# A Strassen-Winograd MLP in fp32: product 5 of the first layer halved once more, and its inner weight sums listed in a stream of their own

## The chip, the core and the metric

The kernel runs on one core of a Trainium2 chip. TensorE (PE) multiplies matrices, VectorE (DVE) and GpSimd (POOL) add tensors, ScalarE (ACT) copies and applies functions, SyncE (SP) issues the DMAs that move data between HBM and the core's SBUF. Matmuls write into the banks of PSUM, and DVE and ACT read them from there. The metric is the device time of one execution in microseconds (us); the median of several runs is given, and lower is better.

## What is computed

Performer attention on q, k, v (8 batches, 8 heads, 576 rows of 64), then a Fourier mixing, then a layer norm and an MLP with a hidden width of 2048. All of it is in fp32. Cut to what matters here:

```
x  = attention(q, k, v, omega)              # (8, 576, 512)
u  = x + real(fft(fft(x, axis=1), axis=2))
un = (u - mean(u)) / sqrt(var(u) + 1e-6)
out = u + maximum(un @ w_ch1, 0) @ w_ch2    # 512 -> 2048 -> 512
```

The last line is 4608 rows (tokens) through two matrix products. The change lies in the first of them, `un @ w_ch1`.

## The kernel before, in words

Up to about 421 us the kernel does the attention and the mixing, and the first 512 tokens of the MLP plainly. The other 4096 tokens go through the MLP in eight blocks of 512, j = 0 to 7, from 421 us to the end. Each block has a first layer and a second one.

**Two levels of halving.** A layer's product of two matrices is cut into 2 x 2 halves and done with seven products in place of eight, after Strassen and Winograd: the operands are sums of halves, and the results are added up into the four cells C11, C12, C21, C22 of the result. These are the outer products, numbered 1 to 7. In the first layer they are done in the order `ORDER1 = (1, 6, 5, 2, 7, 3, 4)`, in block 0 in `ORDER0 = (1, 2, 6, 5, 7, 3, 4)`. Each outer product is either

- done "twice" halved: it is itself cut into 2 x 2 halves and done as seven leaves of four matmuls 128 x 128 x 128 (line L1454 in the first layer, L1815 in the second), with inner sums of its weights and of its tokens; or
- done "single": four quarters of four matmuls with 256 columns each (L1586), with no inner sums.

`single(j)` says which. In block 0 all products but the first are single, in blocks 1 to 7 only product 5 is. The second layer is done twice halved throughout.

**What a product of the first layer leaves.** `hid` holds the four cells, each of 2 x 2 tiles of 128 x 512. For a product of leaves, ACT saves partial results (L1479) and copies seeds into banks (L1486), and DVE adds bank and saved part into a cell (L1497, L1401, L1506, L1477). For a single product, ACT copies each quarter's bank into the cell (L1540), and product 5's quarter has one more user: `u4_of`, DVE at L1550, adds bank and C21 into C12, and only then is the bank free. That sum, C12 = C22 + C21, is called u4 here. Product 7's and 3's results are added onto it.

**Sums on SBUF tiles.** All of them are written by a helper, `add`, and have one line, L1419. It lets the planner choose POOL or DVE. Through it go the sums of hidden cells (`hid<-hid`), the sums of hidden tiles for the second layer's leaves (`sums`, three buffers a product, of which the first is used a second time), the outer weight sums `so5`, `so6`, `so3` and the one for product 7, which replaces a part of `w1` in place, and the inner weight sums.

**The inner weight sums.** Each twice halved outer product i of the first layer needs four sums of the quarters of its outer weights: s1, s2, s4, and one that replaces the quarter a21 in place. s1, s2 and s4 are written into a ring of four spare buffers in `rx` and stored to DRAM from there, as `w1l` (L1674, 256 KB each). Every block from 1 on loads them again as `wx` (L1712), in turn with the second layer's leaf weights `wl<-w2l` (L1721), through 12 buffers. The function `w1_sums` lists all of this in one stream: first the outer sums, then for each product in `ORDER0`, as soon as block 0 has done that product's matmuls (a wait for `("first", 0, i)`), its four inner sums. Before block 1's token sums for such products are listed, `token_sums(1)` waits for all the stores.

**What sets the order.** The instructions of each engine are put down in an order that a planner (`Listing.run`) works out ahead of time. It takes steps from several streams (`halves` with the products and their sums, `load_leaves`, `late_norms`, `late_turns`, `w1_sums` ...), each step with an engine, an assumed duration, waits, and a due time made of `due(j, layer, i)` and a `bias`. Of the steps that could begin at about the earliest time it takes the one that is due first. In its model DVE and POOL never add on SBUF operands at the same time. The order thus fixed is run as it stands: each engine does its list in order, and waits on semaphores for what others make. The DMAs named here are all issued from SP's queue, in the order of its list.

In the second layer the outer products go in the order 4, 1, 2, 6, 5, 3, 7. Their results are collected in `part` (L1793 on DVE, L1835 and L1857 on ACT), and added onto the residual `ur` (L1864, POOL or DVE). The tokens of the next block are normed meanwhile (POOL at L1045 to L1047), turned (DVE, L984), stored as `turned` and loaded as `unT` (L1000).

Of the kernel before, what the change touches and what calls it, by code (L numbers as in the profile page):

```python
# [15 lines left out]
ALU = mybir.AluOpType  # L16
# [20 lines left out]
PE, ACT, DVE, POOL, SP, NONE = "pe", "act", "dve", "pool", "sp", "none"  # L37
# [255 lines left out]
def kernel(  # L293
# [10 lines left out]
    nc = tc.nc  # L304
# [880 lines left out]

    def single(j):

        return (5,) if j else ORDER0[1:]

    def twice(j):  # L1190
        return tuple(i for i in ORDER1[1:] if i not in single(j))
# [27 lines left out]
    def token_sums(j):  # L1219
        if j == 1:  # L1220
            yield Step(NONE, after=tuple(("w1l", i, n) for i in twice(1) for n in (5, 6, 3)))
        for i in twice(j):
            for m, op in enumerate(inner_tokens(j, i)):
                yield Step(
                    DVE, 0.28, after=(("tt", j),), makes=("tokens", j, i) if m == 3 else None, port=True,
                    bias=due(j, 0, i) - 5.0,
                )
                op()
# [94 lines left out]
    def sums_left(a11, a12, a21, a22, s1, s2, s4):  # L1323

        return (
            (s1, a21, a22, ALU.add),
            (s2, s1, a11, ALU.subtract),
            (a21, a11, a21, ALU.subtract),
            (s4, a12, s2, ALU.subtract),
        )  # L1330
# [13 lines left out]
    def weights_of(j, i, n):  # L1344
        if i == 1 and n in (5, 6, 3, 7):
            return w1s[:, (5, 6, 3, 7).index(n)]
        if n in (1, 2, 4, 7):
            d, f = {1: (0, 0), 2: (1, 0), 4: (1, 1), 7: (0, 1)}[n]
            return outer_weights(i)[:, d, GW * f : GW * f + GW]
        return wxs[j, i, n]  # L1350
# [54 lines left out]
    def cell_of(c, f, t):  # L1405
        return hid[:, c, f, t]
# [7 lines left out]
    def add(o, l, r, op, engines=(POOL, DVE), **kw):  # L1414
        n = math.prod(o.shape[1:]) / 512
        step = Step({e: {POOL: 1.3, DVE: 0.65}[e] * n + 0.05 for e in engines}, port=True, **kw)
        yield step
        eng = nc.gpsimd if step.eng == POOL else nc.vector
        eng.tensor_tensor(out=o, in0=l, in1=r, op=op)  # L1419
# [5 lines left out]
    def first_of(j, i):  # L1425
# [91 lines left out]
        def last_cell(f, t):  # L1517
            o = cell_of(C22, f, t)
            after = ("h", j, 7, f, t), ("h", j, "u4", f, t)
            yield from add(o, o, cell_of(C21, f, t), ALU.add, after=after, makes=("h", j, "sum", f, t), bias=due(j, 0, 4) - due(j, 0, 5) - 1)  # L1520
            yield Step(ACT, 0.6, 0.1, makes=made(f, t))
            nc.scalar.activation(out=o, in_=o, func=AF.Relu)  # L1522

        if i == 5:
            for f in range(2):
                for t in range(2):
                    yield Fork(last_cell(f, t))
        bank = ("bank",)
        if i in single(j):
            def cells(n, f, c):  # L1530
# [112 lines left out]
    def w1_sums():  # L1643

        a = {n: outer_weights(n) for n in (1, 2, 7, 4)}
        for i in (2, 4):
            for d in range(2):
                for f in range(2):
                    yield Step(NONE, makes=("sum", i, d, f))

        def part(w, d, f):
            return w[:, d, GW * f : GW * f + GW]

        spare = rx[:].rearrange("p i n b q -> p (i n b q)")

        def inner(m, i):
            raw = [weights_of(0, i, n) for n in (1, 2, 7, 4)]
            new = {}
            for k, n in enumerate((5, 6, 3)):
                at = (3 * m + k) % 4 * GW  # L1660
                new[n] = spare[:, at : at + GW]
            ops = sums_left(*raw, *(new[n] for n in (5, 6, 3)))
            for k, (o, l, r, op) in enumerate(ops):
                n = (5, 6, 7, 3)[k]
                turn = 3 * m + (0, 1, 2, 2)[k] - 4
                free = (("stored", turn),) if n != 7 and turn >= 0 else ()
                yield from add(o, l, r, op, (POOL, DVE), after=free, makes=("wx", 0, i, n) if n != 7 else ("so", i, 7), bias=due(1, 0, i) - 40)
            for k, n in enumerate((5, 6, 3)):
                yield Fork(stored(i, 3 * m + k, n, new[n]))

        def stored(i, turn, n, w):
            after = ("wx", 0, i, n), ("wx", 0, i, {5: 6, 6: 3}.get(n, n))
            yield Step(SP, 0.5, 2.5, after=after, kb=256, makes=("stored", turn))
            nc.sync.dma_start(w1l[i][(5, 6, 3).index(n)], w)  # L1674
            yield Step(NONE, makes=("w1l", i, n))

        parts = (0, 1), (0, 0), (1, 0), (1, 1)
        def outer(i, l, r, op, user):
            for d, f in parts:
                yield from add(  # L1680
                    *(part(w, d, f) for w in (outer_weights(i), l, r)), op, (POOL, DVE), makes=("sum", i, d, f),
                    bias=due(0, 0, user) - 6,
                )

        yield Step(NONE, after=(("us", B - 1), "converted"))
        yield from outer(5, a[7], a[4], ALU.add, 6)
        yield from outer(6, so[5], a[1], ALU.subtract, 6)
        yield Step(NONE, after=tuple(("op", n) for n in range(NPLAIN)))
        yield from outer(7, a[1], a[7], ALU.subtract, 7)
        yield from outer(3, a[2], so[6], ALU.subtract, 3)  # L1690
        for m, i in enumerate(i for i in ORDER0 if i in twice(1)):
            yield Step(NONE, after=((("first", 0, i), "leaves"),))
            yield from inner(m, i)
            for n in (1, 2, 4):
                yield Step(NONE, makes=("so", i, n))
# [9 lines left out]
    def load_leaves():  # L1705
        for j in range(NTB):
            for i in twice(j):
                for n in (5, 6, 3):
                    yield Step(SP, 0.45, 2.6, take=("wl",), after=(("w1l", i, n),), kb=165, makes=("wx", j, i, n),
                               bias=due(j, 0, i) - 14)  # L1710
                    wx = late.tile([128, GW], F32, name="wx", tag="wl", bufs=NWL)
                    nc.sync.dma_start(wx[:], w1l[i][(5, 6, 3).index(n)])  # L1712
                    wxs[j, i, n] = wx
            for i in order(j):
                for l in PARTS:
                    yield Step(
                        SP, 0.45, 2.6, take=("wl",), after=(("w2l", i),), kb=165, makes=("wl", j, i, l),
                        bias=due(j, 1, i) - 14,
                    )
                    wl = late.tile([128, 4, 128], F32, name="wl", tag="wl", bufs=NWL)  # L1720
                    nc.sync.dma_start(wl[:].rearrange("p f m -> p (f m)"), w2l[i][STORED.index(l)])  # L1721
                    wls[j, i, l] = wl
# [190 lines left out]
    def due(j, layer, i):  # L1913
        order_ = order(j) if layer else ORDER1 if j else ORDER0
        return LEAF * (98 * j + 49 * layer + 7 * order_.index(i))
# [4 lines left out]
    def wash():  # L1920

        yield Step(POOL, 0.5)
        zero = late.tile([P, DM], BF16, name="junk", tag="junk", bufs=1)
        nc.gpsimd.memset(zero[:], 0.0)
        taken = []
        for i in range(len(CLEAN)):
            yield Step(PE, 0.25, take=("clean",))
            b, ps = got()
            taken.append(b)
            nc.tensor.matmul(ps, lhsT=zero[:, 0:128], rhs=zero[:], start=True, stop=True)  # L1930
        yield Step(NONE, give=tuple(taken), makes="washed")

    def halves():
        yield Step(NONE, after=("washed",))
        for j in range(NTB):
            for i in ORDER1 if j else ORDER0:
                yield Step(NONE, take=("set",))
                yield Fork(first_of(j, i), due(j, 0, i))
            yield Fork(read_up(j))
            yield Fork(left_sums(j), 0.0)  # L1940
            cells = {}
            yield Fork(second_of(j, cells))
            for i in order(j):
                yield Step(NONE, take=("set",))
                yield Fork(product_of(j, i, cells), due(j, 1, i))

    def late_norms():
        for j in range(1, NTB):
            yield from block_norms(j, late)

    def late_turns():
        for j in range(1, NTB):
            yield from normed(j, late)

    listing.run([wash(), late_turns(), late_norms(), halves(), load_leaves(), token_sums(0), w1_sums()])


# [28 lines left out]
```

## Time and profile before

| what | value |
|---|---|
| median of 3 runs | 1149.73 us (1147.95 to 1150.81) |
| profiled execution | 1150.66 us, span 1148.9 us, mean granted clock of PE 0.996 |
| PE busy | 1125.8 us, 98% |
| DVE busy | 875.2 us, 76% |
| ACT busy | 542.7 us, 47% |
| POOL busy | 410.5 us, 36% |
| DMA | 219 GB/s in the mean over the span |

The profile is one execution, taken by the hardware profiler. A row of a timeline or of the chain begins with its start in us from the span's begin and its length; rows of one kind that follow each other are drawn together ("x24" are 24 of them), and what stands in brackets is the idle time before it and what ended that. A fp32 matmul gives two records, so a leaf of four matmuls shows as x8. PE's records are modelled at their ends and overlap by a little, so the pitch from one start to the next is the time of a leaf, not the length of its row. A row of a table by windows gives the window, its length, the busy time and the number of instructions of PE, PE's weight loads, DVE, ACT and POOL, then the granted clock of PE (1.00 is full), the DMA share and GB/s. "Issue" as a releaser means that the profile shows no event that ended the wait. Names of tiles are the program's: `sums` are the second layer's sums, `wl` its weights, `tt` and `unT` tokens of the first layer, `so` and `w` its weights.

### The profile page before, as it was taken

How to read it: one execution, taken by the hardware profiler on the slowest of the kernel's cores; microseconds unless marked ns; L12 is line 12 of the kernel's file. 1: busy time of each engine (PE TensorE's matmuls, PEld its weight loads, DVE VectorE, ACT ScalarE, POOL GpSimd, SP SyncE). 2: the span in 40 equal slices, each digit the busy share in tenths (PEclk: the TensorE clock that was granted, in tenths of full speed). 3: DMA queues.
4: the chain of work that ended last, by engine and by line, in shares of the span. 5: the costliest groups of instructions: out<-in, count | busy, mean ns of one | idle time of the engine just before them, and what ended most of it. 6: DMA issues, size and time to landing. Idle time of an engine off the chain costs nothing.

```text
span 1148.9 us, 33814 instructions
## 1 busy us (share of the span) xinstructions
PE 1125.8 (98%) x13472; PEld 1042.1 (91%) x13472; DVE 875.2 (76%) x1704; ACT 542.7 (47%) x1639; POOL 410.5 (36%) x420
## 2 busy tenths in 40 slices
PE   8999999999999999989999999999999999999998
PEld 7888888879878868989999999999999999999998
DVE  6999899987676645487787777777678688678676
ACT  7998898856444227614424423423423422522311
POOL 2443444455471206720610610520430440340171
PEclk9999999999999999989999999999999999999999
DMA  7866766675663255686796697698598698598476
GB/s 237 233 188 186 212 197 177 194 228 166 204 192 109 86 152 161 202 290 224 230 341 214 197 338 232 184 300 272 170 297 286 178 286 294 181 269 294 146 217 206
DMA packets 184508, 251.97 MB, mean 219 GB/s; under 512 B 52000, under 2 KB 82976, under 8 KB 184352
## 3 DMA queue, kind: packets, MB, share of 16 engines
q1 hardware_dynamic: 183856, 249.56, 70.3%
q8 instruction: 107, 1.75, 0.6%
q14 instruction: 49, 0.40, 0.1%
q10 hardware_dynamic: 496, 0.26, 0.1%
HBM read 206.77 MB, written 47.19 MB: 221 GB/s over the span
## 4 chain that ended last, share of the span: by engine, by line
PE 54%; DMA 3%; issue 1%; DVE 0%; POOL 0%; ACT 0%; SPq 0%; DVEq 0%; POOLq 0%
PE banks L1815 27%; PE banks L1454 23%; PE banks L1586 4%; DMA wl<-w2l 1%; DMA unT<-turned 1%; DVE sums L1419 0%; POOL rstd L1046 0%; ACT u L1049 0%; POOL rstd L1045 0%; DVE part L1793 0%; SPq L1721 0%; SPq L1000 0%; DVE ur L1747 0%; ACT part L1857 0%; ACT banks L1831 0%
## 5 line engine op out<-in xcount | busy, mean ns | idle before, releaser
L1815 PE MATMUL banks<-wl,sums 128*128 128x128 f32 x1792 | 221.6, 277 | 5.2 <-issue 4.8
L1815 PEld LDWEIGHTS banks<-wl,sums 128*128 128x128 f32 x1792 | 211.8, 194 | 5.9 <-issue 5.0
L578 ACT ACTIVATE e<-banks,nmx 128x128 f32<-128x128 f32 x576 | 165.4, 438 | 22.8 <-DVE nmx L561 22.2
L1815 PE MATMUL banks<-wl,hid 128*128 128x128 f32 x1344 | 170.9, 276 | 2.8 <-DMA wl<-w2l 1.4
L1815 PEld LDWEIGHTS banks<-wl,hid 128*128 128x128 f32 x1344 | 160.1, 192 | 4.2 <-ACT s L1788 1.4
L1419 POOL TENSOR_TENSOR hid<-hid 128x512 f32<-128x512 f32 x76 | 100.6, 1335 | 60.3 <-DVE hid L1497 54.9
L561 DVE TENSOR_REDUCE nmx<-banks 128x8 f32<-128x1024 f32 (+1 forms) x96 | 89.3, 951 | 17.2 <-PE banks L618 13.0
L1788 ACT ACTIVATE s<-banks 128x128 f32<-128x128 f32 x112 | 31.1, 277 | 126.0 <-PE banks L1815 109.1
L1864 POOL TENSOR_TENSOR part<-part 128x512 f32<-128x512 f32 x8 | 10.6, 1325 | 223.3 <-ACT part L1857 190.5
L618 PE MATMUL banks<-om,kqT 64*64 64x128 f32 (+1 forms) x2088 | 79.3, 275 | 2.2 <-ACT kv L668 1.5
L1793 DVE TENSOR_TENSOR part<-banks,s 128x128 f32<-128x128 f32 x112 | 32.2, 289 | 58.8 <-PE banks L1815 58.3
L618 PEld LDWEIGHTS banks<-om,kqT 64*64 64x64 f32 (+1 forms) x2088 | 64.7, 138 | 13.5 <-issue 4.1
L1419 DVE TENSOR_TENSOR sums<-hid 128x512 f32<-128x512 f32 x95 | 74.6, 786 | 1.5 <-ACT hid L1522 1.5
L1454 PE MATMUL banks<-rx,wx 128*128 128x128 f32 x560 | 74.0, 275 | 0.0
L1497 DVE TENSOR_TENSOR hid<-banks,s 128x512 f32<-128x512 f32 x58 | 40.1, 691 | 37.1 <-PE banks L1454 36.0
L1454 PEld LDWEIGHTS banks<-rx,wx 128*128 128x128 f32 x560 | 68.2, 192 | 0.0
L1127 PE MATMUL banks<-unT,w 128*128 128x128 f32 x512 | 65.4, 279 | 1.7 <-DVE qeT L538 1.7
L1586 PE MATMUL banks<-tt,so 128*128 128x256 f32 x288 | 66.3, 379 | 0.0
L467 POOL TENSOR_TENSOR w<-w,raw 128x512 f32<-128x512 f32 x28 | 37.5, 1349 | 77.8 <-DVE raw L461 77.8
L1419 DVE TENSOR_TENSOR hid<-hid 128x512 f32<-128x512 f32 x84 | 59.9, 760 | 6.2 <-ACT hid L1540 6.2
L1127 PEld LDWEIGHTS banks<-unT,w 128*128 128x128 f32 x512 | 60.2, 192 | 4.5 <-issue 2.3
L1401 DVE CUSTOM_DVE_ANT_0 hid<-banks,s 128x512 f32<-128x512 f32 x63 | 43.4, 690 | 26.2 <-PE banks L1454 23.2
(194 smaller groups left out, 2398.9 us busy)
## 6 DMA issues: line engine op xcount, KB each, us to landing
wl<-w2l SPq DMA_DIRECT2D x392, 256.0 KB, 5.1
wx<-w1l SPq DMA_DIRECT2D x105, 256.0 KB, 4.1
raw<-in_moe_w_ch_dram SPq DMA_DIRECT2D x32, 512.0 KB, 4.3
kq<-in_k_dram SPq DMA_DIRECT2D x32, 288.0 KB, 4.8
kq<-in_q_dram SPq DMA_DIRECT2D x32, 288.0 KB, 4.6
vd<-in_v_dram SPq DMA_DIRECT2D x32, 288.0 KB, 5.4
u<-us SPq DMA_DIRECT2D x36, 256.0 KB, 2.5
ur<-us SPq DMA_DIRECT2D x36, 256.0 KB, 4.2
```

What stands on the lines that cost most here:

```text
L467: eng.tensor_tensor(out=dst, in0=dst, in1=lof, op=ALU.add)
L561: nc.vector.tensor_reduce(nmx[:, :, 0:num], pps[:, :, 0 : MF * num].rearrange("p b (c m) -> p b c m", m=MF), axis=AX.X, op=ALU.max, negate ...
L578: nc.scalar.activation(out=e[:, c + (i if num == 1 else 0), :], in_=pps[:, i, MF * c : MF * c + MF], func=AF.Exp, bias=nmx[:, i, c : c + 1],)
L618: nc.tensor.matmul(pps[cols, c, MF * m : MF * m + MF], lhsT=kqT[rows, j, cols], rhs=om2[rows, :],)
L1127: nc.tensor.matmul(hp[:, 0:TP], lhsT=w1[:, dc, 128 * fc : 128 * fc + 128], rhs=unTs[key][:, dc, :], start=(dc == 0), stop=(dc == NDC - 1),)
L1401: nc.vector._custom_dve(TENSOR_ADD_SAT, out=o, in0=ps, in1=sb, s0=FMAX, s1=0.0)
L1419: eng.tensor_tensor(out=o, in0=l, in1=r, op=op)
L1454: nc.tensor.matmul(ps[:, P * f : P * f + P].rearrange("f (b q) -> f b q", q=Q), lhsT=left[:, P * f : P * f + P], rhs=right, start=start an ...
L1497: nc.vector.tensor_tensor(out=o, in0=ps, in1=kept[saved][:], op=ALU.add)
L1586: nc.tensor.matmul(cell.rearrange("f t (b q) -> f t b q", q=Q), lhsT=w[:, d, col : col + 128], rhs=right[:, :, d].rearrange("f (t b) q -> ...
L1793: nc.vector.tensor_tensor(out=part[:, t, 128 * m : 128 * m + 128], in0=ps[:, 0:128], in1=saved[with_][:], op=ALU.add,)
L1815: nc.tensor.matmul(ps[:, 0:128], lhsT=left[:, f], rhs=wls[j, i, n][:, f], start=start and f == 0, stop=(f == 3), skip_group_check=True,)
```

## The change

Two things are changed.

1. `single(j)` is empty for blocks 1 to 7: product 5 of the first layer is twice halved there too, seven leaves of L1454 in place of four quarters of L1586. With it go three more inner weight sums that are stored and loaded again in each block (18 stores in all in place of 15), one more sum in place, and four token sums a block. C12 = C22 + C21 has no bank to read any more; it becomes four adds of cells, `u4_cell`, on POOL or DVE.
2. The inner weight sums leave `w1_sums` for a stream of their own, `w1_inner`. It takes the products in the order `INNER = (2, 6, 5, 4, 7, 3)`, and no longer waits for block 0's matmuls of the product, only for its outer sums. The sum that replaces a21 in place does wait for those matmuls; it becomes a fork of its own, `replaced`. The due times change from `due(1, 0, i) - 40` to `LEAF * (8 + 7 * m)` for the m-th product, and `LEAF * (30 + 7 * m)` for the one in place.

The planner then works out all the lists anew. On PE 112 matmuls with 256 columns go and 196 with 128 columns come. POOL has 22 more adds of `hid`, and fewer inner weight sums (DVE has most of them now). SP issues 24 more DMAs of 256 KB. Line numbers behind the changed places shift: L1586 becomes L1596, L1550 becomes L1560, L1674 becomes L1711, L1721 becomes L1745, L1793 becomes L1817, L1815 becomes L1839, L1864 becomes L1888; L1419, L1454 and L1497 stay.

```diff
     def single(j):
 
-        return (5,) if j else ORDER0[1:]
+        return () if j else ORDER0[1:]
...
+        def u4_cell(f, t):
+            read = (("second", j - 1, READ["u4"]), "read")
+            yield from add(
+                cell_of(C12, f, t), cell_of(C22, f, t), cell_of(C21, f, t), ALU.add,
+                after=(read, made(f, t), ("h", j, 6, f, t)), makes=("h", j, "u4", f, t),
+                bias=due(j, 0, 7) - due(j, 0, 5),
+            )
+
         if i == 5:
             for f in range(2):
                 for t in range(2):
                     yield Fork(last_cell(f, t))
+                    if i not in single(j):
+                        yield Fork(u4_cell(f, t))
...
+    INNER = (2, 6, 5, 4, 7, 3)
+
+    def w1_inner():
...
-            ops = sums_left(*raw, *(new[n] for n in (5, 6, 3)))
-            for k, (o, l, r, op) in enumerate(ops):
-                n = (5, 6, 7, 3)[k]
-                turn = 3 * m + (0, 1, 2, 2)[k] - 4
-                free = (("stored", turn),) if n != 7 and turn >= 0 else ()
-                yield from add(o, l, r, op, (POOL, DVE), after=free, makes=("wx", 0, i, n) if n != 7 else ("so", i, 7), bias=due(1, 0, i) - 40)
+            s1, s2, a21, s4 = sums_left(*raw, *(new[n] for n in (5, 6, 3)))
+            for k, ((o, l, r, op), n) in enumerate(((s1, 5), (s2, 6), (s4, 3))):
+                turn = 3 * m + k - 4
+                free = (("stored", turn),) if turn >= 0 else ()
+                yield from add(
+                    o, l, r, op, after=free, makes=("wx", 0, i, n), bias=LEAF * (8 + 7 * m),
+                )
             for k, n in enumerate((5, 6, 3)):
                 yield Fork(stored(i, 3 * m + k, n, new[n]))
+            yield Fork(replaced(i, a21))
+
+        def replaced(i, a21):
+            o, l, r, op = a21
+            yield from add(
+                o, l, r, op, after=((("first", 0, i), "leaves"), ("wx", 0, i, 5)), makes=("so", i, 7),
+                bias=LEAF * (30 + 7 * m),
+            )
...
-        for m, i in enumerate(i for i in ORDER0 if i in twice(1)):
-            yield Step(NONE, after=((("first", 0, i), "leaves"),))
+        yield Step(NONE, after=("converted",))
+        for m, i in enumerate(i for i in INNER if i in twice(1)):
+            yield Step(NONE, after=tuple(("sum", i, d, f) for d in range(2) for f in range(2)))
             yield from inner(m, i)
...
-    listing.run([wash(), late_turns(), late_norms(), halves(), load_leaves(), token_sums(0), w1_sums()])
+    listing.run([wash(), late_turns(), late_norms(), halves(), load_leaves(), token_sums(0), w1_sums(), w1_inner()])
```

More of the change, by code (lines that the diff above doesn't have):

```diff
@@ L1652, in part @@
             return w[:, d, GW * f : GW * f + GW]
[L1654 to L1661, printed above, removed]
-            ops = sums_left(*raw, *(new[n] for n in (5, 6, 3)))
-            for k, (o, l, r, op) in enumerate(ops):
-                n = (5, 6, 7, 3)[k]
-                turn = 3 * m + (0, 1, 2, 2)[k] - 4
-                free = (("stored", turn),) if n != 7 and turn >= 0 else ()
-                yield from add(o, l, r, op, (POOL, DVE), after=free, makes=("wx", 0, i, n) if n != 7 else ("so", i, 7), bias=due(1, 0, i) - 40)
[L1668 to L1675, printed above, removed]
         parts = (0, 1), (0, 0), (1, 0), (1, 1)
@@ L1690, in w1_sums, with inner, stored @@
         yield from outer(3, a[2], so[6], ALU.subtract, 3)
-        for m, i in enumerate(i for i in ORDER0 if i in twice(1)):
-            yield Step(NONE, after=((("first", 0, i), "leaves"),))
+    INNER = (2, 6, 5, 4, 7, 3)
+    def w1_inner():
+        spare = rx[:].rearrange("p i n b q -> p (i n b q)")
+        def inner(m, i):
+            raw = [weights_of(0, i, n) for n in (1, 2, 7, 4)]
+            new = {}
+            for k, n in enumerate((5, 6, 3)):
+                at = (3 * m + k) % 4 * GW
+                new[n] = spare[:, at : at + GW]
+            s1, s2, a21, s4 = sums_left(*raw, *(new[n] for n in (5, 6, 3)))
[5 more added lines that the diff above has]
+                )
+            for k, n in enumerate((5, 6, 3)):
+                yield Fork(stored(i, 3 * m + k, n, new[n]))
+            yield Fork(replaced(i, a21))
[5 more added lines that the diff above has]
+            )
+        def stored(i, turn, n, w):
+            after = ("wx", 0, i, n), ("wx", 0, i, {5: 6, 6: 3}.get(n, n))
+            yield Step(SP, 0.5, 2.5, after=after, kb=256, makes=("stored", turn))
+            nc.sync.dma_start(w1l[i][(5, 6, 3).index(n)], w)
+            yield Step(NONE, makes=("w1l", i, n))
+        yield Step(NONE, after=("converted",))
+        for m, i in enumerate(i for i in INNER if i in twice(1)):
+            yield Step(NONE, after=tuple(("sum", i, d, f) for d in range(2) for f in range(2)))
             yield from inner(m, i)
```

## The prediction

> **What bounds the kernel now.** I read the page first, for the busy shares and the shares of the chain that ended last, then what TensorE (PE) waited for from 420 us on, where the blocks begin, then the chain in order of time, and last the timelines of the engines round the one long wait.
>
> ```profile
> PE 1125.8 (98%) x13472; PEld 1042.1 (91%) x13472; DVE 875.2 (76%) x1704; ACT 542.7 (47%) x1639; POOL 410.5 (36%) x420
> ...
> PE 54%; DMA 3%; issue 1%; DVE 0%; POOL 0%; ACT 0%; SPq 0%; DVEq 0%; POOLq 0%
> ```
>
> PE is busy for 98% of the span. What it waits for in the 728 us of the blocks fits in seven lines:
>
> ```profile
> PE banks L1815 <- issue: 4.8, 1, 4.8
> PE banks L1815 <- DMA wl<-w2l: 1.4, 2, 1.3
> PE banks L1815 <- DVE part L1793: 0.9, 2, 0.5
> PE banks L1930 <- POOL junk L1924: 0.8, 1, 0.8
> PE banks L1586 <- ACT banks L1567: 0.5, 1, 0.5
> PE banks L1815 <- ACT s L1788: 0.4, 1, 0.4
> PE banks L1815 <- ACT part L1857: 0.4, 1, 0.4
> ```
>
> They sum to 9.2 us, and one wait is half of it. So there are two ways to save time here: fewer matmuls, or that one wait. The next fences show both. The first is the chain (start, length, what): the first layer of block 1, and the same place of the two blocks behind it.
>
> ```profile
> 614.56 8.04 PE banks L1454 x72
> 622.60 1.73 PE banks L1586 x8
> ...
> 627.84 3.46 PE banks L1586 x16
> 631.29 23.22 PE banks L1454 x208
> ...
> 719.49 23.22 PE banks L1454 x208
> ...
> 809.57 23.22 PE banks L1454 x208
> ```
>
> A leaf is 8 records (4 matmuls, each listed twice), so 72 records in 8.04 us are 9 leaves of 0.893 us. A quarter of product 5 (L1586) takes 1.73 us. A block lasts 88.2 us (719.49 - 631.29); the next one lasts 90.1, 1.9 more. The second fence is PE's timeline at both waits, with PE's and the other engines' busy time, granted clock, DMA share and GB/s in windows behind them:
>
> ```profile
> 492.95 2.08 PE L1815 MATMUL banks<-wl,hid 128*128 128x128 f32 x16
> 499.83 5.35 PE L1815 MATMUL banks<-wl,sums 128*128 128x128 f32 x24 [4.80 <-issue]
> ```
> ```profile
> 500.00:504.00 4.00, 4.00 (x19) 4.00 (x20) 2.20 (x6) 0.00 (x0) 0.00 (x0) 0.50 0.27 76
> 505.00:510.00 5.00, 4.63 (x41) 4.44 (x40) 4.41 (x8) 1.37 (x5) 0.00 (x0) 1.00 0.99 300
> 774.00:777.00 3.00, 2.27 (x20) 2.30 (x21) 1.85 (x4) 0.26 (x1) 0.00 (x0) 1.00 1.04 385
> ```
> ```profile
> 774.73 1.13 PE L1815 MATMUL banks<-wl,hid 128*128 128x128 f32 x8 [1.27 <-DMA wl<-w2l]
> ```
>
> Behind the 4.80 us the granted clock is 0.50 for four microseconds, and 1.00 again from 505. Three leaves (24 records) took 5.35 there; at full clock they are 3 x 0.893 plus the tail of 0.3 that the row of 16 shows, 2.98 at most, so the low clock cost at least 2.4. The wait is therefore worth 7.2 us. A wait of 1.27 (block 3) left the clock at 1.00.
>
> "Issue" names no releaser; VectorE (DVE) and GpSimd (POOL) do:
>
> ```profile
> 428.24 2.48 DVE L1419 TENSOR_TENSOR so<-w 128x512 f32<-128x512 f32 x4
> ...
> 491.76 5.70 DVE L1419 TENSOR_TENSOR hid<-hid 128x512 f32<-128x512 f32 x4
> 497.38 1.74 DVE L1864 TENSOR_TENSOR ur<-ur,part 128x512 f32<-128x512 f32 x1
> 499.05 0.68 DVE L1419 TENSOR_TENSOR sums<-hid,sums 128x512 f32<-128x512 f32 x1
> ```
> ```profile
> 492.15 1.42 POOL L1419 TENSOR_TENSOR rx<-rx,so 128x512 f32<-128x512 f32 x1 [3.91 <-DMA w1l<-rx]
> ...
> 496.88 1.71 POOL L1419 TENSOR_TENSOR rx<-w 128x512 f32<-128x512 f32 x1
> ```
>
> The waiting leaf needs the sum that DVE ends at 499.73. Ahead of it stand four adds and one onto `ur`, 7.3 us for five, though four adds alone took 2.48 (0.62 each) at 428. In just that time POOL does four inner weight sums. Five adds alone would be 3.1, so each POOL instruction cost DVE 1.05.
>
> **The change part by part.**
>
> *Product 5 in seven leaves.* Four quarters are 6.92 us, seven leaves 6.25: 0.67 less in each of blocks 1 to 7, **-4.7**, all on PE, which nothing covers. Sides: it could be 0 if a block is bound by something else, and no more than 4.7.
>
> *The sums C12 = C22 + C21.* They were made by DVE from PSUM; now they are four adds of SBUF cells, and by the instruction list most go to POOL, which gets 22 more adds of `hid`.
>
> ```profile
> L1550 DVE TENSOR_TENSOR hid<-banks,hid 128x512 f32<-128x512 f32 x28 | 19.0, 684 | 12.6 <-ACT hid L1540 12.6
> ```
> ```profile
> 901.23 0.19 POOL L1045 TENSOR_SCALAR rstd<-mv 128x1 f32<-128x1 f32 x1 [9.68 <-ACT junk L1041]
> ...
> 907.08 1.28 POOL L1419 TENSOR_TENSOR hid<-hid 128x512 f32<-128x512 f32 x1 [4.75 <-DVE hid L1497]
> ```
>
> They land where POOL stands idle today (9.68 and 4.75 us in block 4) and cost it 4 x 1.28 = 5.1 per block. What takes them is product 7's result, some 13 leaves (11.6 us) later in the list. DVE loses four instructions of 684 ns and gains two PSUM adds and four token sums for product 5. I cost this at **0**, covered by POOL's idle time; if that cover were gone, they would be 5.1 us late at most, still inside those 13 leaves. DVE runs on PSUM operands meanwhile.
>
> *Three more loads of 256 KB a block, and three stores once.* One block, and one second layer alone:
>
> ```profile
> 898.16:986.59 88.43, 88.43 (x763) 87.46 (x762) 67.76 (x124) 31.59 (x78) 26.07 (x29) 1.00 0.81 251
> 925.86:969.85 43.99, 43.99 (x394) 43.84 (x394) 36.62 (x75) 10.29 (x34) 6.90 (x6) 1.00 0.97 308
> ```
>
> 0.79 MB at the 385 GB/s of 774 are 2.0 us of DMA time, and the block has 19% of 88.4 us free, 16.8. They are issued on SP's queue, in order, ahead of the loads for product 7's leaves, in a first layer where the queue has room. I take **0**; ends: -1.4 (the two DMA waits vanish, since the turned tokens of the next block are asked for about a leaf earlier against PE) and +2.0 in each block (the rival below).
>
> *Inner weight sums early, block 0's first layer.* DVE gets four more sums ahead of product 7's weights and of C12 (the rows of before are these):
>
> ```profile
> 430.65 4.65 DVE L1419 TENSOR_TENSOR so<-so,w 128x512 f32<-128x512 f32 x4
> 435.21 6.79 DVE L1419 TENSOR_TENSOR w<-w 128x512 f32<-128x512 f32 x4
> 441.93 1.28 DVE L1550 TENSOR_TENSOR hid<-banks,hid 128x512 f32<-128x512 f32 x2
> ```
> ```profile
> 443.79 6.21 PE L1586 MATMUL banks<-tt,so 128*128 128x256 f32 x28
> 449.83 2.54 PE L1586 MATMUL banks<-unT,w 128*128 128x256 f32 x11
> ```
>
> POOL's sums for product 2 move to 421, before DVE is busy, so its outer sums for 3 end near 438 as now. DVE: three inner sums slowed (3 x 1.1) from 435.3, then the four of `w` without POOL (2.5), one more (0.6) and C12: 442.4, against 442.6 now. The quarter that needs C12's bank starts near 446, product 7 at 449.83. **0**, with 3.5 us of slack; if the first sums' ring buffers were not stored in time, these three queue behind that wait on DVE, and PE behind them (a rival). The other new DVE sums fall into later idle time of DVE, the last stores long before block 1. SP issues in order too: each of the 18 stores waits there for its sum. By the list, 12 `wl` loads stand ahead of all but three of them, and the loads behind are wanted six leaves or more after the last sum that could hold them, so that is **0** as well, at most one landing late (7.2 with the clock, as in rival C).
>
> *The wait at 495.* The POOL sums that slowed DVE are gone from there, and the add onto `ur` goes elsewhere: by the list the last sum of product 6 now follows three adds and one onto `ur`, two microseconds ahead of its leaf. **-7.2**; ends -4.8 (the 2.4 of the clock come back elsewhere) and -7.2.
>
> *What is late next.* The same kind of sum, for product 2, twelve microseconds earlier:
>
> ```profile
> 483.02 0.29 DVE L1793 TENSOR_TENSOR part<-banks,s 128x128 f32<-128x128 f32 x1 [0.53 <-PE banks L1815]
> ```
> ```profile
> 485.75 1.27 POOL L1419 TENSOR_TENSOR sums<-hid,sums 128x512 f32<-128x512 f32 x1 [0.45 <-PE banks L1815]
> ```
>
> Today POOL makes it by 487.0. In the changed list it is DVE's, behind four adds, an in-place weight sum and an add onto `ur`, all after the add at 483.02-483.31: seven times 0.62 is 4.3, so 487.6. Its leaf is due near 486.6 (one leaf sooner than now). Floor: 1.0 us. Two POOL instructions (an add onto `ur`, a C21 sum) run in that time; at 1.05 each, 3.1. Ceiling: all seven at the 1.42 of the row at 491.76, 493.3, a wait of 6.7 and the low clock, 9.1. I take **+3.1**, as these POOL adds have the form of those at 492, and no clock loss: 3.1 stands as far from 1.27 as from 4.80, and a floor of 1.0 draws it down.
>
> [...]
>
> Sum against the profiled 1150.66 (span 1148.9 and 1.76 around it): -4.7 - 7.2 + 3.1 = -8.8, so 1141.9. The median is 0.93 below that execution, which makes **1141**.
>
> **The rivals.**
>
> *A, the stall only moves (0.2).* The wait for product 2 grows to 5 us and the clock halves: +7.4 in place of 3.1, only the PE gain left. For: the ceiling above, and that 3.1 lies between a wait with and one without the drop. Against: only two POOL instructions there, not four. 1150.66 - 4.7 - 7.2 + 7.4 - 0.93 = 1145.
>
> [...]
>
> *B, all of it goes well (0.12).* The wait is the floor of 1.0 and the DMA waits go: 1150.66 - 4.7 - 7.2 + 1.0 - 1.4 - 0.93 = 1137. For: POOL's two adds may fall after the chain. Against: both wait for things ready by 486.
>
> *C, block 0's first layer stalls too (0.1).* DVE's sums wait for stores to free the ring, or POOL slows more than 3.5 us of them; product 5 or 7 then waits about as long as the leaf at 499, clock included: 1141 + 7.2 = 1148. Against: the first stores are issued near 425, ten microseconds before.
>
> *D, slower: the DMA engines become the bound (0.1).* The place is every block: a share of 0.97 over a second layer says that its loads come just in time. If the three loads push them back for good, each block lasts 88.4 + 2.0 and PE's 0.67 is lost as well: 1141 + 7 x 2.7 = 1160. It decides from 1.8 us a block (8.8 + 3.4 over seven). Against: 0.81 over the block, 251 GB/s where 385 were had.
>
> **How the numbers follow.** The forecast has 0.48. Within 0.3%, or 3.4 us, the measurement could not tell a change; that is from 1146.3 to 1153.2. Faster: the forecast, B, and three quarters of A, 0.75. Same: the rest of A and most of C, 0.12. Slower: D and a bad C, 0.13. The range reaches from below B (1135) to above C (1151) and leaves D and the tails out; the forecast's own is 1138 to 1144.
>
> **What would show it.** Right: no quarters (L1586) from block 1 on and 56 more leaf records in each; blocks of 87.6 us; no wait above 1 us near 495-500; one of 1 to 3.5 near 487 on L1815 with DVE's sums ahead of it and a granted clock of 1.00; POOL adds of `hid` in block 4 near 890-900. Wrong: a clock of 0.5 behind 487 (A), waits on L1586 at 446-450 (C), waits for `wl<-w2l` or `wx<-w1l` in each block (D).

## The result and the profile after

| | before | changed |
|---|---|---|
| median of 5 runs each | 1149.73 us (1147.95 to 1151.4) | 1138.29 us (1136.59 to 1139.8) |
| ratio, 95% interval | | 0.990 (0.9883 to 0.9917) |
| profiled execution | 1150.66 us, span 1148.9 | 1138.29 us, span 1136.3 |
| PE busy | 1125.8 us | 1116.1 us |

The change makes the kernel 1.0% faster, 11.4 us; 8.7 were forecast. The medians of before lie between 1149.7 and 1152.6 from one set of runs to the next, so the sets are compared by their ratios to the runs of before beside them.

What PE waits for from 420 us on, in the changed kernel, has four lines in place of seven:

```profile
PE banks L1839 <- issue: 3.2, 1, 3.2
PE banks L1954 <- POOL junk L1948: 1.0, 1, 1.0
PE banks L1596 <- ACT banks L1577: 0.5, 1, 0.5
PE banks L1839 <- DVE part L1817: 0.4, 1, 0.4
```

They sum to 5.1 us, 9.2 before. The one large wait sits where the prediction put it. The timelines of PE, DVE and POOL round it:

```profile
486.70 1.06 PE L1839 MATMUL banks<-wl,sums 128*128 128x128 f32 x8
490.97 2.02 PE L1839 MATMUL banks<-wl,sums 128*128 128x128 f32 x16 [3.21 <-issue]
```
```profile
484.43 2.49 DVE L1419 TENSOR_TENSOR hid<-hid 128x512 f32<-128x512 f32 x4
486.84 1.76 DVE L1419 TENSOR_TENSOR so<-so 128x512 f32<-128x512 f32 x1
488.52 1.75 DVE L1888 TENSOR_TENSOR ur<-ur,part 128x512 f32<-128x512 f32 x1
490.19 0.68 DVE L1419 TENSOR_TENSOR sums<-hid,sums 128x512 f32<-128x512 f32 x1
```
```profile
486.36 1.68 POOL L1888 TENSOR_TENSOR ur<-ur,part 128x512 f32<-128x512 f32 x1 [4.05 <-DVE hid L1419]
488.00 1.71 POOL L1419 TENSOR_TENSOR hid<-hid 128x512 f32<-128x512 f32 x1
```

The four adds take 0.62 each; POOL is idle up to 486.36. The next two instructions of DVE take 1.76 and 1.75, about as long as POOL's two beside them (1.68 and 1.71). The leaf waits for the sum that ends at 490.87.

From block 1 on PE has one wait, of 0.38 us in the last block. The chain of the changed kernel has the same long stretch at these places, blocks 1, 2, 4 and 6:

```profile
521.95 39.31 PE banks L1454 x352
...
609.50 39.31 PE banks L1454 x352
...
784.59 39.31 PE banks L1454 x352
...
959.68 39.31 PE banks L1454 x352
```

A block lasts 87.55 us (609.50 - 521.95, and half of 959.68 - 784.59): 98 leaves of 0.893. Before, the stretches from block 1 to block 7 were these:

```profile
542.20 24.12 PE banks L1454 x216
...
1074.99 23.22 PE banks L1454 x208
```

From the end of the first (566.32) to the end of the last (1098.21) are six blocks of 88.65 us in the mean, where 91 leaves and four quarters are 88.2. So before lost 2.7 us there (6 x 0.45), and the profile after loses nothing. Two waits for loads of `wl`, 1.27 and 0.16, are the part of the 2.7 that the list of waits names; the rest are gaps too short for that list (the leaf at 766.97 starts 0.30 late), and what a wait costs beyond its listed length (with the wait of 1.27, two leaves take 3.30, from 772.40 to 775.70, where 1.79 is their length).

### The profile page after: what moved, and what is told of

Its sections match the earlier page's. It is cut to its first block, busy times and chain, and to the rows that moved or that the text cites. A ratio compares the mean times of both kernels' runs of the same rounds, so it can differ in the third digit from the quotient of the medians.

```text
span 1136.3 us, 34262 instructions
## 1 busy us (share of the span) xinstructions
PE 1116.1 (98%) x13639; PEld 1039.7 (91%) x13640; DVE 871.9 (77%) x1735; ACT 544.6 (48%) x1646; POOL 423.5 (37%) x435
## 4 chain that ended last, share of the span: by engine, by line
PE 92%; DVE 2%; DMA 2%; ACT 2%; issue 1%; SPq 0%; POOL 0%; DVEq 0%; POOLq 0%
PE banks L1839 31%; PE banks L1454 27%; PE banks L618 5%; PE banks L1127 5%; PE banks L524 5%; PE banks L1150 4%; PE banks L1596 4%; PE banks L652 3%; PE banks L699 2%; PE banks L861 2%; PE banks L811 1%; DMA kq<-in_q_dram 1%; PE banks L821 1%; PE banks L872 1%; ACT e L578 1%
## 5 line engine op out<-in xcount | busy, mean ns | idle before, releaser
L1839 PE MATMUL banks<-wl,sums 128*128 128x128 f32 x1792 | 219.0, 275 | 3.3 <-issue 3.2
L1839 PEld LDWEIGHTS banks<-wl,sums 128*128 128x128 f32 x1792 | 209.3, 192 | 3.7 <-issue 3.7
L1419 POOL TENSOR_TENSOR hid<-hid 128x512 f32<-128x512 f32 x98 | 128.8, 1318 | 118.7 <-ACT hid L1511 66.5
L1839 PE MATMUL banks<-wl,hid 128*128 128x128 f32 x1344 | 170.4, 275 | 0.4 <-DVE part L1817 0.4
L1839 PEld LDWEIGHTS banks<-wl,hid 128*128 128x128 f32 x1344 | 160.1, 192 | 0.6 <-DVE part L1817 0.6
L1454 PE MATMUL banks<-rx,wx 128*128 128x128 f32 x672 | 88.8, 275 | 0.0
L1497 DVE TENSOR_TENSOR hid<-banks,s 128x512 f32<-128x512 f32 x72 | 49.8, 691 | 42.9 <-PE banks L1454 35.6
L1454 PEld LDWEIGHTS banks<-rx,wx 128*128 128x128 f32 x672 | 81.8, 192 | 0.0
L1817 DVE TENSOR_TENSOR part<-banks,s 128x128 f32<-128x128 f32 x112 | 32.2, 289 | 48.6 <-PE banks L1839 47.0
L1479 ACT ACTIVATE s<-banks 128x512 f32<-128x512 f32 x65 | 38.7, 595 | 57.4 <-PE banks L1454 56.9
L1477 DVE TENSOR_TENSOR s<-banks,hid 128x512 f32<-128x512 f32 x70 | 48.4, 692 | 19.7 <-PE banks L1454 17.5
L1855 ACT ACTIVATE banks<-banks 128x128 f32<-128x128 f32 x56 | 14.7, 262 | 96.5 <-PE banks L1839 93.9
L1419 DVE TENSOR_TENSOR hid<-hid 128x512 f32<-128x512 f32 x90 | 57.5, 683 | 4.5 <-ACT hid L1550 4.5
```

The costliest lines, as they stand in the source:

```text
L1454: nc.tensor.matmul(ps[:, P * f : P * f + P].rearrange("f (b q) -> f b q", q=Q), lhsT=left[:, P * f : P * f + P], rhs=right, start=start an ...
L1477: nc.vector.tensor_tensor(out=s[:], in0=ps, in1=cell_of(addend, f, t), op=ALU.add)
L1497: nc.vector.tensor_tensor(out=o, in0=ps, in1=kept[saved][:], op=ALU.add)
L1839: nc.tensor.matmul(ps[:, 0:128], lhsT=left[:, f], rhs=wls[j, i, n][:, f], start=start and f == 0, stop=(f == 3), skip_group_check=True,)
```

## The experiments

**Each part alone.** First the moved weight sums with product 5 single as before:

```diff
     def single(j):
 
-        return () if j else ORDER0[1:]
+        return (5,) if j else ORDER0[1:]
```

> The second part of the change alone: the inner weight sums in their own early stream, product 5 single as before. My sum: the PE term comes back, 7 x 0.67 = 4.7, so 1138.3 + 4.7 = 1143.0; the wait of about 3 us near 488 stays, nothing at 495. If the DMA waits that went with the change (blocks 3 and 4, with the small ones about 2.7 us) belong to product 5, they come back too and it is 1143 to 1145.7. Rival, that all the gain comes from the moved sums: 1138 to 1139.

Measured: 1146.86 us, ratio 0.9976 (0.9964 to 0.9988), so 2.8 us of gain. The long wait near 495 is gone, but other waits have come, of sums and of loads:

```profile
PE banks L1839 <- DVE sums L1419: 2.2, 2, 1.2
PE banks L1839 <- DMA wl<-w2l: 2.1, 1, 2.1
PE banks L1839 <- ACT s L1812: 1.2, 1, 1.2
PE banks L1839 <- DVE part L1817: 0.9, 2, 0.5
```

The wait of 3 us near 488 that was expected isn't in it: its list is another, with 1.22 there. The time lies 1.2 us above the upper end of what was expected, and the way to it is another. The rival, that the moved sums bring all of the gain, is out.

Then the other half: product 5 in leaves, with the inner sums in `w1_sums` as before.

```diff
     def single(j):
 
-        return (5,) if j else ORDER0[1:]
+        return () if j else ORDER0[1:]
...
+        def u4_cell(f, t):
...
                     yield Fork(last_cell(f, t))
+                    if i not in single(j):
+                        yield Fork(u4_cell(f, t))
```

> The first part alone: product 5 in seven leaves, C12 by four adds, the inner weight sums listed where they were before. My sum: 1149.7 - 4.7 = 1145.0, with a wait of 4 to 6 us in block 0's second layer near 495 and a granted clock near 0.5 behind it; 1142.3 if the DMA waits of blocks 3 and 4 go with product 5. Rival, that the wait goes with product 5 and not with the sums: 1138 to 1141.

Measured: 1145.67 us, ratio 0.9962 (0.9949 to 0.9975), 4.4 us of gain. That is near the number expected, and once more not the way. The timelines of PE, DVE and POOL and, last, the chain:

```profile
532.12 2.08 PE L1454 MATMUL banks<-rx,wx 128*128 128x128 f32 x8 [7.94 <-DVE rx L1217]
```
```profile
490.11 2.49 DVE L1419 TENSOR_TENSOR hid<-hid 128x512 f32<-128x512 f32 x4
492.51 0.69 DVE L1874 TENSOR_TENSOR ur<-ur,part 128x512 f32<-128x512 f32 x1
493.11 0.69 DVE L1419 TENSOR_TENSOR sums<-hid,sums 128x512 f32<-128x512 f32 x1
...
531.78 0.29 DVE L1217 TENSOR_TENSOR rx<-tt 128x128 f32<-128x128 f32 x1 [5.96 <-DMA w1l<-rx]
```
```profile
495.96 1.27 POOL L1419 TENSOR_TENSOR rx<-rx,w 128x512 f32<-128x512 f32 x1 [8.65 <-DMA w1l<-rx]
```
```profile
516.99 7.09 DMA u<-us
524.08 0.02 issue
524.10 7.65 DMA w1l<-rx
531.75 0.02 issue
531.78 0.30 DVE rx L1217
```

The chain of four adds, one onto `ur` and the sum takes 3.7 us here (490.11 to 493.80); before it took 8.0 (491.76 to 499.73). In this run POOL waits 8.65 us for a ring buffer and adds nothing in that time. So the 4.8 us were POOL's sums beside DVE's adds, as read.

But block 1 is held up now. Its token sums wait for the last store, which lands at 531.75, and PE waits 7.94 us, with a granted clock of 0.50 from 532 to 536. The three stores more are only a part of this: the profile of before has the first of these token sums at 531.41, nearly as late, but there PE came to the first leaf on `rx` and `wx` only at 534.11, and here it is there at 524.2. The wait near 495 had hidden how late the stores end. The parts alone are worth 2.8 and 4.4; together they gave 11.4. Without the early sums block 1 waits for their stores, and with them alone the list has the other waits shown above, 6.4 us in the four lines.

**The wait near 488.** If it is DVE's chain, a shorter chain must shorten it. First the in-place sums are due later:

```diff
-                bias=LEAF * (30 + 7 * m),
+                bias=LEAF * (60 + 7 * m),
```

> The change with one due time moved: the weight sums in place (a21) are due 30 leaves later, so the one on so3 no longer stands ahead of the last sum of product 2 on DVE. My theory, that the wait near 488 is DVE's chain of adds: it shrinks by the 1.76 us of that instruction to about 1.4 and the time is 1136.5, or down to 0 and 1135 if the list changes more. Rival, that something else releases the leaf (issue): the wait stays at 3.2 and the time at 1138.3.

Then the sum is given to POOL, as before the change:

```diff
-                yield from add(o, l, r, op, after=after, ...)
+                yield from add(o, l, r, op, (POOL,) if (j, i, n) == (0, 2, 3) else (POOL, DVE), after=after, ...)
```

> The change with the last sum of product 2 in block 0's second layer on POOL, as it was before the change. My theory: the wait of 3.2 near 488 goes, 1138.3 - 3.2 = 1135.1, and no wait above 1 us is left in the blocks. Rival, that POOL's adds then slow another chain of DVE: the wait moves to a sum a few us later, 1137 to 1138.5.

Measured: 1138.41 and 1138.30 us, both with the ratio 0.9904 (0.989 to 0.9917 and 0.9888 to 0.9919). The wait of 3.2 is gone from both, so it was DVE's chain, and neither is faster. The rivals' mechanisms were wrong too: PE now waits for loads in the main. PE's waits with the sum due later, then with the sum on POOL:

```profile
PE banks L1839 <- DMA wl<-w2l: 3.4, 3, 1.9
```
```profile
PE banks L1839 <- DMA wl<-w2l: 2.6, 2, 1.5
PE banks L1839 <- DVE turn L984: 0.9, 1, 0.9
```

**What paces block 0's second layer.** The new theory: the DMA engines. To test it, half of the weights of three products are left out of the loads in block 0:

```diff
-                    nc.sync.dma_start(wl[:].rearrange("p f m -> p (f m)"), w2l[i][STORED.index(l)])
+                    part = slice(0, 256) if j == 0 and i in (2, 6, 5) else slice(0, 512)
+                    nc.sync.dma_start(wl[:].rearrange("p f m -> p (f m)")[:, part], w2l[i][STORED.index(l)][:, part])
...
-                    rhs=wls[j, i, n][:, f],
+                    rhs=wls[j, i, n][:, f % 2 if j == 0 and i in (2, 6, 5) else f],
```

> The kernel with product 2's last sum on POOL, and with half of the weights of products 2, 6 and 5 of block 0's second layer left out of the loads (their matmuls read the other half twice, so these results are not the reference's). The theory since the runs before, that the DMA engines set the pace of that layer once DVE's wait is gone: the waits of 2.6 us for weights and 0.9 for the turned tokens go, 1138.3 - 3.3 = 1135.0. Rival, that the order in SP's queue or DVE makes these waits: 1138.

> The change with the same half of the weights of products 2, 6 and 5 of block 0 left out of the loads (results not the reference's), product 2's last sum on DVE as in the change. My theory, that the wait of 3.2 near 488 is DVE's chain of adds and not the loads: it stays at 3.2 and the time at 1138.3. Rival, that the loads are behind that wait too: it goes, 1135.

Measured: 1135.47 us, ratio 0.9867 (0.9843 to 0.9891), with the sum on POOL, and 1138.72, ratio 0.9898 (0.9875 to 0.992), with the sum on DVE. In the first the waits for loads are gone, in the second the wait of 3.21 is there to the hundredth. A window over block 0's second layer, first of the changed kernel, then with the sum on POOL, then with half the loads besides (the third figure from the end is the clock, the next the DMA share):

```profile
480.00:508.00 28.00, 24.65 (x219) 24.33 (x218) 24.84 (x44) 5.69 (x20) 5.46 (x5) 1.00 1.05 316
```
```profile
480.00:508.00 28.00, 25.48 (x222) 24.80 (x221) 23.91 (x42) 6.40 (x22) 3.46 (x3) 1.00 1.06 313
```
```profile
480.00:508.00 28.00, 26.48 (x235) 26.10 (x234) 26.49 (x47) 6.34 (x22) 3.98 (x4) 1.00 0.86 253
```

So two things hold PE up in that layer, each for about 3 us (3.2 for DVE in the change, 3.4 and 2.6 for loads without that wait), and they overlap: while PE waits for DVE, the loads catch up. From 488 to 492 they move 388 GB/s in the changed kernel, with PE busy for 1.03 us of the four, and PE waits for no load in that profile. Taking away one of them is worth nothing. Both are worth about 3 us in the medians, though the interval with both overlaps the other two at its edge. In the profiles PE's waits from 420 us on sum to 5.1 us in the change, 5.4 with the sum on POOL, 4.9 with half the loads and 3.2 with both. A version that keeps all loads and adds a buffer for them was tried, since in the first layer of block 0 the DMA engines have room (a share of 0.35 between 460 and 470):

```diff
-    NWL, NSUM = 12, 3
+    NWL, NSUM = 13, 3
...
-            s = late.tile([128, 4 * P], F32, name="s", tag="s", bufs=6)
+            s = late.tile([128, 4 * P], F32, name="s", tag="s", bufs=5)
```

> The kernel with product 2's last sum on POOL, and 13 buffers for the loads of weights rather than 12 (one of the six buffers of saved partial results is given up for it). The theory that the DMA engines set the pace of block 0's second layer: one leaf more is loaded ahead in the first layer, where they have room, so the waits of 2.6 us for weights shrink by up to 0.9 and the time is 1136 to 1137.4; a wait for a saved result (L1479) may come in its place, then 1138 or more.

Measured: 1138.21 us, ratio 0.9869 (0.985 to 0.9888), beside 0.988 (0.9862 to 0.9899) of the change in the same set: not told apart. One load is still waited for 2.2 us, and a sum on DVE for 1.5. Why the buffer more doesn't help is open.

**The loads in blocks 1 to 7.** Behind the `wx` loads of two products, or of product 5 alone, come as many copies that nobody reads:

```diff
                     nc.sync.dma_start(wx[:], w1l[i][(5, 6, 3).index(n)])
+                    if i in (5, 2):
+                        nc.sync.dma_start(again[j % 2, i, n][:], w1l[i][(5, 6, 3).index(n)])
```

> The change with six further DMAs of 256 KB in the first layer of each of blocks 1 to 7 (copies of the inner weight sums of products 5 and 2 from DRAM to DRAM, which nobody reads): twice as many again as the change added, and two buffers' reads of them in the queue. My theory, that the first layers have room for them: 1138.3, at most 1 us more. Rival D, that the loads push the second layer's loads back: 6 x 262144 bytes at 385 GB/s are 4.1 us a block, 28.6 in all, 1167; half of it if half is hidden, 1152.

> The change with three further DMAs of 256 KB in the first layer of each of blocks 1 to 7, half of the six that cost 12 us. If the price is a threshold (the load of the next block's tokens comes too late for ScalarE, which then holds a seed that PE waits for): 1138 to 1140, and ScalarE's waits for these tokens are longer without PE waiting. If it is in proportion, half of 12: 1144.

Measured: six more a block 1150.02 us, ratio 0.9994 (0.9978 to 1.0011); three more 1141.29 us, ratio 0.9897 (0.9878 to 0.9916) beside 0.988 of the change. Six cost about 11 us, three about 2, which the intervals don't tell from nothing: nearer to a threshold than in proportion. With three PE waits once for a seed, 0.54 us, and the clock fell behind its wait near 488 (see below), so even the 2 us need not be the loads. My expectation for six, at most 1 us, was wrong, and so was rival D's place. The waits with six are in the first layers of blocks 2, 4 and 6, and on ScalarE (PE's waits, PE's and ACT's timelines in block 2, and the chain there):

```profile
PE banks L1454 <- ACT banks L1486: 8.2, 3, 3.5
```
```profile
622.68 1.48 PE L1454 MATMUL banks<-tt,so 128*128 128x128 f32 x8 [2.02 <-ACT banks L1486]
```
```profile
620.58 0.63 ACT L1036 ACTIVATE junk<-u 128x512 bf16<-128x512 f32 x1 [3.26 <-DMA u<-us]
...
622.05 0.58 ACT L1486 ACTIVATE banks<-banks 128x512 f32<-128x512 f32 x1
```
```profile
613.08 7.47 DMA u<-us
```

The load of the next block's rows (`u`) takes 7.47 us behind the copies. ACT's norm waits for it, and the seed of a bank that PE needs stands behind that norm in ACT's list.

**The clock behind the wait.** The waiting sum was written three times, which draws the wait out by two adds:

```diff
+                if (j, i, n) == (0, 2, 3):
+                    for _ in range(2):
+                        nc.vector.tensor_tensor(out=o, in0=l, in1=r, op=op)
```

> The change with the last sum of product 2 in block 0's second layer written three times on DVE rather than once, the same value each time: the wait near 488 is drawn out by two adds, 3.2 + 1.2 = 4.4 us. If the clock falls behind 4.4 us as it did behind 4.80: 1138.3 + 1.2 + 2.4 = 1141.9, with a granted clock near 0.5 behind 492. If it holds as it did behind 3.21: 1139.5.

Measured: a wait of 4.66 us, a granted clock of 0.50 for four microseconds behind it, 1139.83 us, ratio 0.991 (0.9892 to 0.9929). The clock fell, but the time is 2.1 us below the 1141.9 that was expected for that; by time alone it can't be told from the change. The change itself was run again:

> The change as it is, on the same chip as the two others. 1138.3 again; behind the wait of 3.21 us near 488 the clock may hold, as in its first profile, or fall, as in the runs with more and with half the loads that had the same wait. If it falls, this run is about 1.4 us above the first.

Measured: 1139.35 us, ratio 0.988 (0.9862 to 0.9899). The clock held behind its 3.21 us, as in the first profile. But in three other profiles with this same wait it fell. Windows behind the wait, of the change, of the change again, with half the loads, with six and with three more loads:

```profile
491.00:493.00 2.00, 2.00 (x18) 2.00 (x19) 1.26 (x3) 0.00 (x0) 0.00 (x0) 1.00 1.04 382
```
```profile
491.00:493.00 2.00, 1.59 (x14) 1.62 (x15) 1.26 (x4) 0.00 (x0) 0.00 (x0) 1.00 0.95 324
```
```profile
492.00:494.00 2.00, 2.00 (x11) 2.00 (x11) 0.90 (x3) 0.00 (x0) 0.00 (x0) 0.50 0.00 2
```
```profile
490.00:492.00 2.00, 2.00 (x12) 2.00 (x12) 0.73 (x3) 0.00 (x0) 0.00 (x0) 0.56 0.97 319
```
```profile
490.00:492.00 2.00, 2.00 (x11) 2.00 (x11) 0.87 (x3) 0.00 (x0) 0.00 (x0) 0.50 1.04 389
```

## Why the prediction was right

- **Product 5 in leaves, -4.7: right.** Blocks of 87.55 us, 87.6 forecast; 0.67 less in each of seven.
- **C12 on POOL, 0: right.** No wait of PE in blocks 1 to 7 has these adds behind it.
- **Block 0's first layer, 0: right.** PE has no wait there beyond the 0.5 that it had before.
- **The wait at 495, -7.2: right.** The wait is gone, and the undisturbed chain of 3.7 us shows its cause; the size of this term by itself no run shows. That only the moved sums would remove it was too narrow: product 5's leaves alone removed it too, since the lists came out otherwise, and put 7.94 us in front of block 1.
- **What is late next, +3.1: right.** It is 3.21, at the forecast place, from the forecast chain. POOL's two adds cost DVE 1.07 and 1.06 (1.76 and 1.75, where such a row takes 0.69 undisturbed at 492.51), 1.05 taken. In these rows the two engines hold each other up: POOL's own take 1.68 and 1.71 there, where its add at 485.75 of before, with DVE idle for most of it, took 1.27.
- **No loss of clock behind it: held in both profiles of the change, and by luck.** It fell in three of the five profiles with that wait. What it costs is seen in the leaves behind the wait. The first two take 2.02 us in the change, and with half the loads this:

```profile
490.94 3.50 PE L1840 MATMUL banks<-wl,sums 128*128 128x128 f32 x16 [3.21 <-issue]
```

  1.5 us more. Over the first four leaves the fall costs 1.5 with half the loads, 1.6 with six more loads and 2.9 with three more (5.12, 5.28 and 6.57 us, against 3.64 in the change). The term can therefore be 3.2 to 6.1 from one execution to the next. In the ten runs of the change the mean granted clock is 0.999 or 1.000 in three, the two profiled ones among them, and 0.997 or 0.998 in seven; so the clock may well have fallen in most of them, but no trace of those shows where.
- **The loads in a block, 0, with an end at -1.4: this term was mis-sized, and other short waits were left out.** From block 1 to block 7 the profile of before loses 2.7 us, the first profile of the change nothing; this is the piece of rival B that came true. The short waits of block 0 (0.39 and 0.37) and one of block 7 (0.51) stand in the prediction's list but not in its sum, and in that profile they went as well. From the first quarter of block 0 to the end the first profile of the change is 13.6 us shorter (720.8 to 707.2), the second 11.4 (709.4), where 8.8 were forecast. How much of the rest belongs to the change stays open: in the second profile one block is 1.5 us longer again. And the stretch ahead of that first quarter, which the change hardly touches, ends between 425.97 and 429.08 in the 13 profiles, so 1 or 2 us between the spans of two single profiles say little.
- **Rival D** has the right resource and the wrong place and size. The change's own three loads a block cost nothing that its blocks of 87.55 us show. Three further ones cost about 2 us, not told from nothing, six further ones 11, through ACT's list in the first layer and not through the second layer's loads.

What I had missed wholly is that the wait for DVE in block 0 hides a wait for DMA of nearly its length. It didn't change the forecast; it would have made a forecast for the obvious next step wrong, and did (1135 and 1136.5 expected, 1138.3 and 1138.4 measured). In the prediction's fences the rows at 614 to 631 belong to block 2, and those at 898 to 987 to block 5, counted from block 1 at 542; no term hangs on it.

## What to carry to other kernels

A wait at the top of a list of waits is worth its length only if the resource next in line isn't late too: look at the DMA share in the same stretch before counting on it (1.05 here, and the 3.2 us of wait were worth nothing). A change of the schedule is not a sum of its parts: run each alone, and read where the wait went, since one half here gave the expected number by another way and the other missed it (4.4 and 2.8 us alone, 11.4 together). And a load that only feeds the next block can stop PE in this one, if an in-order engine has something urgent behind it: with six more loads ACT waited 3.26 us for the next block's `u`, and PE 2.02 us for the seed behind it.

## What the runs showed of the hardware that I had not expected

The fall of the clock isn't set by the length of the wait alone. Behind 4.66, 4.80 and 7.94 us of idle PE the granted clock went to 0.50. Behind the same 3.21 us it fell in three profiles and held in two. With six more loads it fell behind 2.02 us (0.83 in the mean from 620 to 630). Behind the two other waits of that run only the leaves show it: 32 of them take 30.48 us behind 3.51, and 28.85 behind 2.69, where 32 of 0.893 are 28.6. With the moved sums alone it fell behind 2.08 us, from 504 on:

```profile
503.57 1.82 PE L1839 MATMUL banks<-wl,hid 128*128 128x128 f32 x8 [2.08 <-DMA wl<-w2l]
```
```profile
504.00:506.00 2.00, 2.00 (x11) 2.00 (x11) 0.00 (x0) 0.26 (x1) 0.00 (x0) 0.50 1.05 383
```

With 13 buffers it held behind 2.22 us (eight records took 1.16, 1.82 in the row above):

```profile
510.50 1.16 PE L1839 MATMUL banks<-wl,hid 128*128 128x128 f32 x8 [2.22 <-DMA wl<-w2l]
```

What else sets it, no run shows: the wait of 3.21 us ended either way, and so did shorter ones, 2.02 and 2.08 with a low clock behind them, 2.22 without. For an estimate of a wait between 2 and 3.5 us I would now carry both cases, some 1.5 to 2.9 us apart, which is what the fall cost behind the 3.21.
